# The last four chunks' expert lists: 24 list columns held stationary while the one-hot rows move

## The chip, the cores and the metric

The kernel runs on one core of a Trainium2 chip. The time is the device time of one execution in microseconds (us), the median of three runs. The core has a matrix engine (TensorE, PE in the profile; its weight loads are PEld), a vector engine (VectorE, DVE), a scalar engine (ScalarE, ACT), GpSimd (POOL) and SyncE (SP), which here only starts transfers. Each works through its own queue in order and waits on semaphores for the others.

## The reference

A gated linear attention makes one row of 384 numbers for each of 3072 tokens; a top-1 mixture of eight experts then works on these rows.

```python
for t in range(S):                      # attention; B, H, S, D = 4, 8, 768, 48
    S_re, S_im = (ar * S_re - ai * S_im) + kv, ar * S_im + ai * S_re
    y[:, :, t] = np.einsum('bhd,bhde->bhe', q[:, :, t], S_re)
x = y.transpose(0, 2, 1, 3).reshape(B * S, H * D)        # 3072 x 384

logits = x @ w_gate                                      # experts; E = 8, F = 1024
e_idx = np.argmax(logits, axis=1)
gate_w = softmax(logits)[np.arange(N), e_idx]
eom = 1.0 / (1.0 + np.exp(-(x @ w_output_gate)))
for e in range(E):
    mask = e_idx == e
    h = np.maximum(x[mask] @ w1[e], 0.0)
    out[mask] = gate_w[mask, None] * eom[mask, e, None] * (h @ w2[e])
```

## The kernel before, in words

Tokens are handled in 24 chunks of 128. The first half of the program is the attention; the second half computes the experts, in the order of how many tokens they hold, on fixed capacities of 464 rows for the first down to 384 for the last.

**Lists.** Each expert needs the list of its tokens: for each place (slot) in it the token's number and its gate. `choose` finds a token's expert and its rank in that expert's list, `weigh` its gate (two exponentials on ACT and six small operations on DVE). For the first 20 chunks the pair is scattered into a table in DRAM and read back into `slots` (four tiles of 116 slots for each expert) and `whole` (three tiles of 128 slots for the last expert). The last four chunks (`T0` onward) come too late for this way. Their part is added with matmuls, in `add`: `hot` is a one-hot matrix of 128 tokens by 464 slots for each chunk, `lhs` holds 24 columns for each token (for each expert the number, and the gate in a high and a low part), and their product, summed over the four chunks, is what `slots` and `whole` still lack. Then `slot_ids` makes the row numbers `sid`, and `gather` fetches the second expert's rows by them: four indirect transfers that POOL issues.

**Where it stands in the program.** All this happens while the first expert (expert 0) is being computed; its rows are put together by another way (`fill`) and need no list. An expert takes eight steps `ft`. A step has nine matmuls of 464 columns into `up` (L1235), from which ACT makes `hh` (L1239) and DVE makes `hl` (L1240), then nine into three accumulators `acc` (L1172): for each accumulator two that read `hh` and one that reads `hl`. The steps are shifted: the nine of `acc` for step n come behind the nine of `up` for step n+1. I call them up0, up1, acc0, up2, acc1 and so on. Meanwhile the next expert's weights arrive in pieces of 768 KB (`raw`, two buffers), and are split into a high part on ACT (L210) and a low part on DVE (L211). A `raw` buffer is free, and SP starts the next transfer, when DVE has made its third low part. The next expert's rows are transposed late in the expert (`xt`, L94).

The generator `lists` is advanced by one `yield` after each step of expert 0, so where it yields decides between which instructions of ACT and DVE its work is put: on these two engines the order is that of the program. On PE the order around expert 0 is chosen by the scheduler from the dependences.

```python
if loaded and e == 0:
    next(last, None)
    if ft == 3:
        over(lpool, lambda: ps.tile([P, 512], F32, name="yp", bufs=1))
```

Here `last` is `lists`, and `over` is a small test whether some expert holds more tokens than its capacity (one matmul L1390, one transpose). The list matmuls and `over` share one bank of PSUM, `yp`.

Of the kernel before, what the change touches and what calls it, by code (L numbers as in the profile page):

```python
# [10 lines left out]
F32 = mybir.dt.float32  # L11
F32R = mybir.dt.float32r
# [4 lines left out]
ALU = mybir.AluOpType  # L17
# [4 lines left out]
P = 128  # L22

CAPS = (464, 440, 424, 416, 408, 400, 392, 384)
CAP = max(CAPS)
# [9 lines left out]
def tile_gated_attention_moe(  # L35
# [216 lines left out]

    def choose(pool, bank, c0, n, tag=""):
        def small(name, shape, dt=F32):
            return pool.tile([P] + shape, dt, name=name + tag)
        gl = logits[:, c0:c0 + n, 0:E]
# [84 lines left out]
    def attention(wctx):  # L341
        with ExitStack() as actx:
# [404 lines left out]
            def place(c0, n):  # L747
                pool = ready["pool"]
                steps = choose(pool, bank, c0, n, tag=str(c0))
                next(steps)  # L750

                ohp = pool.tile([P, n, E], F32, name=f"ohp{c0}")
# [4 lines left out]
                dl, oh = at_once(steps)  # L757
                tail["choice", c0] = dl, oh, ohp
                for c in range(c0, c0 + n):
# [5 lines left out]

            def add(pool, bank):
                lp = bank()
                new = lp[:, :NS * 3 * E].rearrange("p (s x) -> p s x", x=3 * E)
                new_whole = lp[:, NS * 3 * E:(NS + KT) * 3 * E].rearrange("p (k x) -> p k x", x=3 * E)
                for i in range(NS):  # L770
                    for c in range(T0, NT):
                        nc.tensor.matmul(
                            new[:NP, i, :], tail["hot", c][:, i * NP:(i + 1) * NP], lhs[:, c - T0, :],
                            start=(c == T0), stop=(c == NT - 1))
                for c in range(T0, NT):
                    whole_hot = pool.tile([P, KT, NS, P // NS], F32R, name="whole", bufs=2)
                    nc.vector.tensor_scalar(
                        out=whole_hot,
                        in0=iota.rearrange("p (b n) -> p b n", b=NS)[:, :, :KT * P // NS].rearrange(
                            "p b (k a) -> p k b a", k=KT),  # L780
                        scalar1=rank[:, c:c + 1], scalar2=None, op0=ALU.is_equal)
                    for k in range(KT):
                        nc.tensor.matmul(
                            new_whole[:, k, :], whole_hot[:, k].rearrange("p b a -> p (b a)"),
                            lhs[:, c - T0, :], start=False, stop=(c == NT - 1), skip_group_check=True)
                for x in range(3):
                    at = slots[:NP, :, :, int(x > 0)]
                    nc.vector.tensor_tensor(
                        out=at, in0=at, in1=new[:NP, :, x * E:(x + 1) * E].rearrange("p s e -> p e s"), op=ALU.add)
                    at = whole[:, :, int(x > 0)]  # L790
                    nc.vector.tensor_tensor(out=at, in0=at, in1=new_whole[:, :, x * E + E - 1], op=ALU.add)

            def gates_of(pool, c0, n):
                dl, oh, ohp = tail["choice", c0]
                for _ in weigh(pool, c0, n, dl, oh, tag=str(c0)):
                    pass
                one = pool.tile([P, n, E], F32, name=f"one{c0}")
                l = lhs[:, c0 - T0:c0 - T0 + n, :]
                nc.vector.tensor_tensor(
                    out=one, in0=ohp, in1=entry[:, c0:c0 + n, 1].unsqueeze(2).broadcast_to([P, n, E]), op=ALU.mult)  # L800
                nc.vector.tensor_copy(out=l[:, :, E:2 * E], in_=one)
                nc.vector.tensor_tensor(
                    out=l[:, :, 2 * E:3 * E], in0=one, in1=l[:, :, E:2 * E].bitcast(F32), op=ALU.subtract)

# [119 lines left out]
            T0 = TAIL[0][0]  # L924
            group_of = {c: c0 for c0, n in TAIL for c in range(c0, c0 + n)}

# [99 lines left out]
            def lists(pool, bank):  # L1026
                for c in range(T0, NT):
                    c0 = group_of[c]
                    hot = tail["hot", c] = pool.tile([P, CAP], F32R, name=f"hot{c}")
                    nc.vector.tensor_scalar(out=hot, in0=iota, scalar1=rank[:, c:c + 1], scalar2=None, op0=ALU.is_equal)  # L1030
                    nc.vector.tensor_scalar(
                        out=lhs[:, c - T0, 0:E], in0=tail["choice", c0][2][:, c - c0, :], scalar1=entry[:, c, 0:1],
                        scalar2=None, op0=ALU.mult)
# [89 lines left out]
    def experts(ready, loaded=False):  # L1123
# [4 lines left out]
        with ExitStack() as ectx:  # L1128
# [93 lines left out]
            for e in range(E):  # L1222
# [5 lines left out]
                for ft in range(FT):  # L1228
# [239 lines left out]
```

## Time and profile before

| | us |
|---|---|
| median of three runs (lowest, highest) | 534.71 (533.62, 534.95) |
| the profiled execution's own time | 535.06 |
| its span, first to last instruction | 533.3 |
| PE busy | 495.2 (93%) |
| DVE busy | 340.6 (64%) |
| ACT busy | 314.2 (59%) |
| POOL busy | 116.3 (22%) |

The span is that of one execution recorded by the hardware profiler. Times in the rows are microseconds from its start. "Idle before" is how long the engine stood still ahead of an instruction, and the name behind the arrow is what it waited for. A row of the timeline merges instructions that follow each other; the end of a matmul is modelled, so the distance between two starts tells more than a row's own length.

### The profile page before, as it was taken

To read this page: it belongs to the slowest core of one execution; us is meant where nothing else is said; L and a number is where in the kernel's file an instruction comes from. 1 tells how busy PE (TensorE), PEld (TensorE's weight loads), DVE (VectorE), ACT (ScalarE), POOL (GpSimd) and SP (SyncE) were. 2 spreads that over 40 slices of the span, in tenths; PEclk is the share of its full clock that TensorE was granted. 3 is DMA by queue.
4 is the path that set the end of the run, shared out by engine and by line. 5 is a ranking of instruction groups with operands and counts; after the bars stand their busy time and mean duration, and the time that the engine had idled before them with its cause. 6 is when DMAs were issued, how large, how long until landed. Compare 5 with 4: busy or idle time off the path is not lost.

```text
span 533.3 us, 10970 instructions
## 1 busy us (share of the span) xinstructions
PE 495.2 (93%) x4191; PEld 427.8 (80%) x4191; DVE 340.6 (64%) x801; ACT 314.2 (59%) x581; POOL 116.3 (22%) x134
## 2 busy tenths in 40 slices
PE   2899896999989999999989899999999999999992
PEld 0378574877877878778787789999999999999992
DVE  5579678998877988898857646444353636355220
ACT  7678677887858789657624236355452726354220
POOL 4002002030110203033310544412334232111112
PEclk9799989999989999999999799999999999999998
DMA  8664542526235321104424565537163544431001
GB/s 285 199 216 137 120 132 61 164 67 179 72 75 149 45 77 49 29 31 135 143 56 145 161 170 180 165 82 235 44 205 120 173 149 142 142 115 50 15 27 45
DMA packets 46898, 63.84 MB, mean 120 GB/s; under 512 B 11769, under 2 KB 38668, under 8 KB 46836
## 3 DMA queue, kind: packets, MB, share of 16 engines
q1 hardware_dynamic: 38708, 53.63, 33.6%
q0 software_dynamic: 8128, 9.42, 6.2%
q8 instruction: 35, 0.57, 0.5%
q14 instruction: 27, 0.22, 0.2%
HBM read 53.92 MB, written 9.88 MB: 120 GB/s over the span
## 4 chain that ended last, share of the span: by engine, by line
PE 59%; issue 16%; DVE 8%; DMA 7%; ACT 5%; POOL 3%; POOLq 0%; SPq 0%; DVEq 0%; ACTq 0%
PE acc L1172 12%; PE up L1235 11%; PE tr L94 6%; PE sc L664 5%; PE cs L574 4%; PE xo L678 4%; PE tr L245 4%; PE cs L521 3%; POOL out_dram L1185 3%; PE xo L684 2%; DMA carry<-ai 2%; PE st L649 2%; DMA xd<-xn 1%; DMA ar<-in_a_re_dram 1%; DMA raw<-in_moe_w_dram 1%
## 5 line engine op out<-in xcount | busy, mean ns | idle before, releaser
L1240 DVE SCALAR_TENSOR_TENSOR hl<-up,hh 128x464 fp32r<-128x464 f32 (+7 forms) x64 | 37.7, 589 | 69.8 <-ACT hh L1239 69.5
L1239 ACT ACTIVATE hh<-up 128x464 fp32r<-128x464 f32 (+7 forms) x64 | 33.0, 516 | 72.5 <-PE up L1235 72.5
L1235 PE MATMUL up<-xh,w1h 128*128 128x464 f32 (+7 forms) x192 | 69.1, 360 | 0.2 <-ACT xh L1022 0.2
L1235 PE MATMUL up<-xl,w1h 128*128 128x464 f32 (+7 forms) x192 | 68.1, 355 | 0.0
L1235 PE MATMUL up<-xh,w1l 128*128 128x464 f32 (+7 forms) x192 | 67.8, 353 | 0.0
L1172 PE MATMUL acc<-hh,w2h 128*128 128x464 f32 (+6 forms) x168 | 61.8, 368 | 0.0
L1172 PE MATMUL acc<-hl,w2h 128*128 128x464 f32 (+6 forms) x168 | 59.8, 359 | 1.5 <-DVE hl L1240 1.5
L1172 PE MATMUL acc<-hh,w2l 128*128 128x464 f32 (+6 forms) x168 | 59.8, 356 | 0.0
L1185 POOL DMA_INDIRECT out_dram<-y,sid x28 | 31.7, 1134 | 125.2 <-ACT y L1207 122.2
L664 PE MATMUL sc<-qt,kt 96*128 96x128 f32 x384 | 52.4, 279 | 0.0
L664 PEld LDWEIGHTS sc<-qt,kt 96*128 96x128 f32 x384 | 47.2, 191 | 3.3 <-issue 1.7
L1116 POOL DMA_INDIRECT rows<-xd,sid x28 | 35.5, 1267 | 57.7 <-DVE w1l L211 29.2
L211 DVE TENSOR_TENSOR w1l<-raw,w1h 128x512 fp32r<-128x512 f32 x48 | 30.7, 685 | 18.9 <-ACT w1h L210 18.8
L678 PE MATMUL xo<-scores,v 128*48 128x128 f32 x384 | 42.7, 279 | 0.0
L211 DVE TENSOR_TENSOR w2l<-raw,w2h 128x512 fp32r<-128x512 f32 x48 | 30.6, 688 | 14.6 <-ACT w2h L210 14.3
L1062 POOL DMA_INDIRECT table<-entry,addr x20 | 28.1, 1404 | 53.5 <-DVE addr L1058 49.3
L1235 PEld LDWEIGHTS up<-xl,w1h 128*128 128x128 f32 x192 | 36.3, 189 | 1.6 <-DVE xl L1023 0.4
L210 ACT CAST w1h<-raw 128x512 fp32r<-128x512 f32 x48 | 27.1, 619 | 17.9 <-DMA raw<-in_moe_w_dram 17.9
L1235 PEld LDWEIGHTS up<-xh,w1h 128*128 128x128 f32 x192 | 36.5, 190 | 1.3 <-ACT xh L1022 0.4
L544 POOL COPY rcs<-rcs 24x48 f32<-24x48 f32 (+2 forms) x10 | 5.4, 540 | 146.2 <-DMA rcs<-re 95.6
L1235 PEld LDWEIGHTS up<-xh,w1l 128*128 128x128 f32 x192 | 36.4, 190 | 1.0
L684 PE MATMUL xo<-qt,state 96*48 96x128 f32 x320 | 36.7, 276 | 0.0
(213 smaller groups left out, 1117.9 us busy)
## 6 DMA issues: line engine op xcount, KB each, us to landing
raw<-in_moe_w_dram SPq DMA_DIRECT2D x32, 768.0 KB
ar<-in_a_re_dram SPq DMA_DIRECT2D x24, 192.0 KB
ai<-in_a_im_dram SPq DMA_DIRECT2D x24, 192.0 KB
k<-in_k_dram SPq DMA_DIRECT2D x24, 192.0 KB
q<-in_q_dram SPq DMA_DIRECT2D x24, 192.0 KB
v<-in_v_dram SPq DMA_DIRECT2D x24, 192.0 KB
xd<-xn SPq DMA_DIRECT2D x24, 192.0 KB
rows<-xd,sid POOLq DMA_INDIRECT x28, 4.3
```

The lines of the kernel that those rows point to most:

```text
L94: return nc.tensor.transpose(out=out, in_=in_, identity=ident[p0:p0 + n, p0:p0 + n])
L211: nc.vector.tensor_tensor(out=lo[:, s], in0=raw[:, s], in1=hi[:, s].bitcast(F32), op=ALU.subtract)
L664: nc.tensor.matmul(sp[:, j * P:(j + 1) * P], r["kt"][:D2, h, :], r["qt"][:D2, h, :], start=True, stop=True)
L678: nc.tensor.matmul(op[u * DP:u * DP + D, j * P:(j + 1) * P], vt[c][:, h * D:(h + 1) * D], r["s"][:, h, :], start=True, stop=(cc == 0))
L684: nc.tensor.matmul(op[u * DP:u * DP + D, j * P:(j + 1) * P], xs[:D2, h * D:(h + 1) * D], r["qt"][:D2, h, :], start=False, stop=True)
L1062: ins = nc.gpsimd.indirect_dma_start(out=table, out_offset=bass.IndirectOffsetOnAxis(ap=addr[:, c:c + 1], axis=0), in_=entry[:, c, :], in_ ...
L1116: ins = nc.gpsimd.indirect_dma_start(out=rows[e % 2][:n, i, :], out_offset=None, in_=xd[:known], in_offset=bass.IndirectOffsetOnAxis(ap=id ...
L1172: nc.tensor.matmul(accs[kt][:, :cap], w[:, cs], a, start=(ft == 0 and s == 0), stop=(ft == FT - 1 and s == 2))
L1185: ins = nc.gpsimd.indirect_dma_start(out=out, out_offset=bass.IndirectOffsetOnAxis(ap=id_of(e, i, n, loaded), axis=0), in_=y[:n, :], in_of ...
L1235: nc.tensor.matmul(up[:, :cap], w[:, kt, :], x[:, kt, :], start=(m == 0), stop=(m == 3 * KT - 1))
L1239: nc.scalar.activation(out=hh, in_=up[:, :cap], func=AF.Relu)
L1240: nc.vector.scalar_tensor_tensor(out=hl, in0=up[:, :cap], scalar=0.0, in1=hh.bitcast(F32), op0=ALU.max, op1=ALU.subtract)
```

## The change

Three things are done. First, the product is taken the other way round: `lhs` is stationary (24 columns) and a chunk's whole one-hot matrix moves (464 columns), four matmuls in place of 28, which leaves the result as 24 rows of 464 slots; these are copied out of PSUM twice (`by_slot` on ACT, and `by_whole`, which puts the last expert's slots in another order, on DVE) and turned by seven small transposes. The one-hot matrices for `whole` (four operations of 128x384 on DVE) go away. Second, the gates of the four chunks, which were computed in groups of two, one and one, are computed together. Third, `lists` has two more places where it yields, and `over` comes one step later. A loop that had four small operations for the first eight columns of `lhs` becomes one operation.

```diff
             def place(c0, n):
                 pool = ready["pool"]
-                steps = choose(pool, bank, c0, n, tag=str(c0))
+                if c0 == T0:
+                    for name in ("dl", "oh", "ohp"):
+                        tail[name] = pool.tile([P, NT - T0, E], F32, name=name + "s")
+                at = {name: tail[name][:, c0 - T0:c0 - T0 + n] for name in ("dl", "oh", "ohp")}
+                steps = choose(pool, bank, c0, n, tag=str(c0), at=at)
...
             def add(pool, bank):
+
+                W3, Q = 3 * E, P // NS
+                sp = bank()
+                for c in range(T0, NT):
+                    nc.tensor.matmul(
+                        sp[:W3, :CAP], lhs[:, c - T0, :], tail["hot", c], start=(c == T0), stop=(c == NT - 1))
+                by_slot = pool.tile([W3, CAP], F32, name="by_slot")
+                by_whole = pool.tile([W3, KT, NS, Q], F32, name="by_whole")
+                nc.scalar.copy(out=by_slot, in_=sp[:W3, :CAP])
+                nc.vector.tensor_copy(
+                    out=by_whole,
+                    in_=sp[:W3, :CAP].rearrange("p (b n) -> p b n", b=NS)[:, :, :KT * Q].rearrange(
+                        "p b (k a) -> p k b a", k=KT))
+                yield
                 lp = bank()
...
                 for i in range(NS):
-                    for c in range(T0, NT):
-                        nc.tensor.matmul(
-                            new[:NP, i, :], tail["hot", c][:, i * NP:(i + 1) * NP], lhs[:, c - T0, :],
-                            start=(c == T0), stop=(c == NT - 1))
-                for c in range(T0, NT):
-                    whole_hot = pool.tile([P, KT, NS, P // NS], F32R, name="whole", bufs=2)
-                    nc.vector.tensor_scalar(
...
-                    for k in range(KT):
-                        nc.tensor.matmul(
-                            new_whole[:, k, :], whole_hot[:, k].rearrange("p b a -> p (b a)"),
-                            lhs[:, c - T0, :], start=False, stop=(c == NT - 1), skip_group_check=True)
+                    turned(out=new[:NP, i, :], in_=by_slot[:, i * NP:(i + 1) * NP])
+                for k in range(KT):
+                    turned(out=new_whole[:, k, :], in_=by_whole[:, k].rearrange("p b a -> p (b a)"))
...
-            def gates_of(pool, c0, n):
-                dl, oh, ohp = tail["choice", c0]
-                for _ in weigh(pool, c0, n, dl, oh, tag=str(c0)):
-                    pass
...
+            def gates(pool):
+                n = NT - T0
+                yield from weigh(pool, T0, n, tail["dl"], tail["oh"], tag="s")
...
             def lists(pool, bank):
...
                 yield
-                for c0, n in TAIL:
-                    gates_of(pool, c0, n)
-                add(pool, bank)
+                for _ in gates(pool):
+                    pass
+                yield
+                yield from add(pool, bank)
                 slot_ids()
...
                         next(last, None)
-                        if ft == 3:
+                        if ft == 4:
                             over(lpool, lambda: ps.tile([P, 512], F32, name="yp", bufs=1))
```

What the program issues moves in three places. The first is PE in the middle of acc1, where the list matmuls begin; `hot_...` is the one-hot matrix of a chunk, `w2h` and `w2l` the two parts of the second weights. Before:

```order
L1172 MATMUL acc<-hh,w2l_3307 128x464
L772 MATMUL yp<-lhs,hot_3836 116x24
L772 MATMUL yp<-lhs,hot_3839 116x24
L1172 MATMUL acc<-hl,w2h_3306 128x464
L1172 MATMUL acc<-hh,w2h_3306 128x464
```

In the changed kernel the four list matmuls stand behind the last matmul of acc1 and ahead of up3:

```order
L1174 MATMUL acc<-hl,w2h_3306 128x464
L774 MATMUL yp<-hot_3830,lhs 24x464
L774 MATMUL yp<-hot_3832,lhs 24x464
L774 MATMUL yp<-hot_3834,lhs 24x464
L774 MATMUL yp<-hot_3836,lhs 24x464
L1237 MATMUL up<-xh_3775,w1h_3302 128x464
```

The first two of 28 list matmuls stood ahead of five matmuls of acc1; now all four stand behind them.

The second is PE in acc2, where before the rest of the list matmuls ran; `whole` is a one-hot matrix for the last expert. Before:

```order
L783 MATMUL yp<-lhs,whole 128x24 x3
L1172 MATMUL acc<-hh,w2h_3306 128x464
L783 MATMUL yp<-lhs,whole 128x24 x3
L1172 MATMUL acc<-hh,w2l_3307 128x464
L1172 MATMUL acc<-hh,w2h_3306 128x464
L1172 MATMUL acc<-hh,w2l_3307 128x464
L1390 LDWEIGHTS ones_b
L1390 MATMUL yp<-run,ones_b 128x8
L1172 MATMUL acc<-hl,w2h_3306 128x464 x3
```

In the changed kernel acc2 is whole, and the transposes stand between it and up4:

```order
L1174 MATMUL acc<-hh,w2h_3306 128x464
L1174 MATMUL acc<-hh,w2l_3307 128x464
L1174 MATMUL acc<-hl,w2h_3306 128x464
L94 MATMUL yp<-ident,by_slot 116x24 x4
L94 MATMUL yp<-ident,by_whole 128x24 x3
L1237 MATMUL up<-xh_3775,w1h_3304 128x464
```

The three matmuls that read `hl` no longer stand at the end of acc2, and `over`'s matmul has moved from inside acc2 to behind acc3.

The third is DVE, between the gates and the making of `sid`. Before, `hl` of step 2 and the rest of the weight split stood behind all of the list work:

```order
L802 TENSOR_TENSOR lhs<-one_3930,lhs 128x8
L777 TENSOR_SCALAR whole<-iota,rank 128x384 x4
L788 TENSOR_TENSOR slots<-slots,yp 116x32
L791 TENSOR_TENSOR whole<-whole,yp 128x3
...
L1095 TENSOR_SCALAR sid<-slots 116x32
L1039 TENSOR_SCALAR whole_sid<-whole 128x3
L1099 COPY gate<-slots 116x32
L211 TENSOR_TENSOR w1l_3849<-raw,w1h_3848 128x512
L211 TENSOR_TENSOR w2l_3853<-raw,w2h_3852 128x512
L1240 SCALAR_TENSOR_TENSOR hl<-up,hh 128x464
```

In the changed kernel they stand right behind the gates:

```order
L805 TENSOR_TENSOR lhs<-ones,lhs 128x4x8
L211 TENSOR_TENSOR w1l_3840<-raw,w1h_3839 128x512
L211 TENSOR_TENSOR w2l_3844<-raw,w2h_3843 128x512
L1242 SCALAR_TENSOR_TENSOR hl<-up,hh 128x464
L779 COPY by_whole<-yp 24x384
L211 TENSOR_TENSOR w2l_3844<-raw,w2h_3843 128x512 x2
L1242 SCALAR_TENSOR_TENSOR hl<-up,hh 128x464
L793 TENSOR_TENSOR slots<-slots,yp 116x32
```

`hl` of steps 2 and 3, and the third low part of the first weight piece, come ahead of the additions to `slots`. On ACT the exponentials of the four chunks shrink from six to two, and `by_slot` stands between `hh` of step 2 and the next two parts of the weight split. On POOL and SP the order is the same.

## Rows read from the trace of the kernel before

**Rows 1.** PE by line, 303.5 to 533.3 us: busy, mean; idle before

```profile
L1235 PE MATMUL up<-xh,w1h 128*128 128x440 f32 (+7 forms) x177 | 62.8, 355 | 0.0
...
L94 PE MATMUL yp<-ident,deep 128*1 128x128 f32 x1 | 0.3, 272 | 0.0
```

**Rows 2.** Timeline of PE, expert 0: start, length, engine, instruction

```profile
279.82 0.48 PE L1235 MATMUL up<-xh,w1h 128*128 128x464 f32 x1 [0.20 <-ACT xh L1022]
...
283.96 0.37 PE L1172 MATMUL acc<-hh,w2h 128*128 128x464 f32 x1
...
288.59 0.37 PE L1172 MATMUL acc<-hh,w2l 128*128 128x464 f32 x1
289.52 0.34 PE L772 MATMUL yp<-lhs,hot 128*116 128x24 f32 x2 [0.56 <-issue]
...
292.86 1.49 PE L772 MATMUL yp<-lhs,hot 128*116 128x24 f32 x13
...
294.88 0.45 PE L1172 MATMUL acc<-hh,w2h 128*128 128x464 f32 x1
...
296.05 0.43 PE L783 MATMUL yp<-lhs,whole 128*128 128x24 f32 x3
...
297.63 0.23 PE L1390 MATMUL yp<-run,ones_b 128*128 128x8 bf16 x1
299.37 1.53 PE L1172 MATMUL acc<-hl,w2h 128*128 128x464 f32 x3 [1.51 <-DVE hl L1240]
...
303.72 0.45 PE L1172 MATMUL acc<-hh,w2h 128*128 128x464 f32 x1
...
305.70 0.37 PE L1235 MATMUL up<-xh,w1h 128*128 128x464 f32 x1
```

**Rows 3.** Windows: length, busy PE PEld DVE ACT POOL, granted clock, DMA, GB/s

```profile
296.00:297.00 1.00, 1.00 (x6) 0.94 (x6) 0.49 (x5) 0.00 (x0) 0.00 (x0) 0.64 0.00 0
...
303.00:304.00 1.00, 1.00 (x6) 0.80 (x5) 0.00 (x0) 1.00 (x2) 0.87 (x1) 0.95 1.05 312
...
317.00:318.50 1.50, 1.50 (x13) 1.38 (x13) 0.00 (x0) 0.48 (x2) 0.11 (x1) 1.00 0.48 149
```

**Rows 4.** Timeline of DVE, expert 0

```profile
287.02 0.64 DVE L1240 SCALAR_TENSOR_TENSOR hl<-up,hh 128x464 fp32r<-128x464 f32 x1 [0.30 <-DMA xd<-xn]
287.58 0.17 DVE L296 TENSOR_TENSOR lo<-oh,logits 128x16 f32<-128x16 f32 x1
...
289.24 0.18 DVE L802 TENSOR_TENSOR lhs<-one,lhs 128x16 fp32r<-128x16 f32 x1
...
297.23 0.18 DVE L1095 TENSOR_SCALAR sid<-slots 116x32 uint32<-116x32 f32 x1
...
297.48 0.68 DVE L211 TENSOR_TENSOR w1l<-raw,w1h 128x512 fp32r<-128x512 f32 x1
```

**Rows 5.** Timeline of PE, the transposes of the second expert's rows

```profile
313.27 0.54 PE L94 MATMUL xt<-ident,rows 110*128 110x110 f32 x4
...
317.45 0.92 PE L94 MATMUL xt<-ident,rows 110*128 110x110 f32 x8
...
318.42 0.36 PE L1235 MATMUL up<-xh,w1l 128*128 128x440 f32 x1
```

**Rows 6.** Timeline of POOL, the second expert's gather, first and fourth

```profile
298.28 1.44 POOL L1116 DMA_INDIRECT rows<-xd,sid  x1 [29.19 <-DVE w1l L211]
...
303.13 1.07 POOL L1116 DMA_INDIRECT rows<-xd,sid  x1 [0.30 <-issue]
```

**Rows 7.** Gathers, issue to landing: the fourth alone, then all 31

```profile
DMA to landing us min/median/max: 4.9/4.9/4.9
...
DMA to landing us min/median/max: 2.9/4.2/11.6
```

**Rows 8.** Timeline of SP: the weight transfers of this stretch

```profile
298.19 2.75 SPq L194 DMA_DIRECT2D raw<-in_moe_w_dram  x2
```

**Rows 9.** Timeline of ACT: the first split of that piece

```profile
303.00 1.14 ACT L210 CAST w1h<-raw 128x512 fp32r<-128x512 f32 x2 [8.42 <-DMA raw<-in_moe_w_dram]
```

More of the change, by code (lines that the diff above doesn't have):

```diff
@@ L251, in gate_logits, with choose @@
             out=logits[:, i, :], in_=part[:, :, D2:].rearrange("p j x -> p x j"), axis=AX.X, op=ALU.add)
-    def choose(pool, bank, c0, n, tag=""):
+    def choose(pool, bank, c0, n, tag="", at=None):
         def small(name, shape, dt=F32):
-            return pool.tile([P] + shape, dt, name=name + tag)
+            return at[name] if at and name in at else pool.tile([P] + shape, dt, name=name + tag)
         gl = logits[:, c0:c0 + n, 0:E]
@@ L748, in place @@
                 pool = ready["pool"]
-                steps = choose(pool, bank, c0, n, tag=str(c0))
+                if c0 == T0:
[3 more added lines that the diff above has]
+                steps = choose(pool, bank, c0, n, tag=str(c0), at=at)
                 next(steps)
-                ohp = pool.tile([P, n, E], F32, name=f"ohp{c0}")
+                ohp = at["ohp"]
                 nc.vector.tensor_tensor(
@@ L756, in place @@
                 yield
-                dl, oh = at_once(steps)
-                tail["choice", c0] = dl, oh, ohp
+                at_once(steps)
                 for c in range(c0, c0 + n):
@@ L767, in add @@
+                nc.vector.tensor_copy(
[3 more added lines that the diff above has]
+                yield
                 lp = bank()
-                new = lp[:, :NS * 3 * E].rearrange("p (s x) -> p s x", x=3 * E)
-                new_whole = lp[:, NS * 3 * E:(NS + KT) * 3 * E].rearrange("p (k x) -> p k x", x=3 * E)
+                new = lp[:, :NS * W3].rearrange("p (s x) -> p s x", x=W3)
@@ L770, in add @@
+                new_whole = lp[:, NS * W3:(NS + KT) * W3].rearrange("p (k x) -> p k x", x=W3)
                 for i in range(NS):
-                    for c in range(T0, NT):
-                        nc.tensor.matmul(
-                            new[:NP, i, :], tail["hot", c][:, i * NP:(i + 1) * NP], lhs[:, c - T0, :],
-                            start=(c == T0), stop=(c == NT - 1))
-                for c in range(T0, NT):
-                    whole_hot = pool.tile([P, KT, NS, P // NS], F32R, name="whole", bufs=2)
-                    nc.vector.tensor_scalar(
[L778 to L781, printed above, removed]
-                    for k in range(KT):
-                        nc.tensor.matmul(
-                            new_whole[:, k, :], whole_hot[:, k].rearrange("p b a -> p (b a)"),
-                            lhs[:, c - T0, :], start=False, stop=(c == NT - 1), skip_group_check=True)
+                    turned(out=new[:NP, i, :], in_=by_slot[:, i * NP:(i + 1) * NP])
@@ L791, in add @@
                     nc.vector.tensor_tensor(out=at, in0=at, in1=new_whole[:, :, x * E + E - 1], op=ALU.add)
-            def gates_of(pool, c0, n):
-                dl, oh, ohp = tail["choice", c0]
-                for _ in weigh(pool, c0, n, dl, oh, tag=str(c0)):
-                    pass
-                one = pool.tile([P, n, E], F32, name=f"one{c0}")
-                l = lhs[:, c0 - T0:c0 - T0 + n, :]
+            def gates(pool):
+                n = NT - T0
+                yield from weigh(pool, T0, n, tail["dl"], tail["oh"], tag="s")
+                one = pool.tile([P, n, E], F32, name="ones")
                 nc.vector.tensor_tensor(
-                    out=one, in0=ohp, in1=entry[:, c0:c0 + n, 1].unsqueeze(2).broadcast_to([P, n, E]), op=ALU.mult)
-                nc.vector.tensor_copy(out=l[:, :, E:2 * E], in_=one)
+                    out=one, in0=tail["ohp"], in1=entry[:, T0:, 1].unsqueeze(2).broadcast_to([P, n, E]), op=ALU.mult)
+                nc.vector.tensor_copy(out=lhs[:, :, E:2 * E], in_=one)
                 nc.vector.tensor_tensor(
-                    out=l[:, :, 2 * E:3 * E], in0=one, in1=l[:, :, E:2 * E].bitcast(F32), op=ALU.subtract)
+                    out=lhs[:, :, 2 * E:3 * E], in0=one, in1=lhs[:, :, E:2 * E].bitcast(F32), op=ALU.subtract)
             FIXED = NT + 9
@@ L924, in attention @@
             T0 = TAIL[0][0]
-            group_of = {c: c0 for c0, n in TAIL for c in range(c0, c0 + n)}
             def rest():
@@ L1027, in lists @@
                 for c in range(T0, NT):
-                    c0 = group_of[c]
                     hot = tail["hot", c] = pool.tile([P, CAP], F32R, name=f"hot{c}")
                     nc.vector.tensor_scalar(out=hot, in0=iota, scalar1=rank[:, c:c + 1], scalar2=None, op0=ALU.is_equal)
-                    nc.vector.tensor_scalar(
-                        out=lhs[:, c - T0, 0:E], in0=tail["choice", c0][2][:, c - c0, :], scalar1=entry[:, c, 0:1],
-                        scalar2=None, op0=ALU.mult)
+                nc.vector.tensor_tensor(
+                    out=lhs[:, :, 0:E], in0=tail["ohp"],
+                    in1=entry[:, T0:, 0].unsqueeze(2).broadcast_to([P, NT - T0, E]), op=ALU.mult)
                 yield
-                for c0, n in TAIL:
-                    gates_of(pool, c0, n)
-                add(pool, bank)
+                for _ in gates(pool):
+                    pass
+                yield
+                yield from add(pool, bank)
                 slot_ids()
```

## The prediction

> **What bounds the kernel now.** I first read PE by line over the second half of the program. From 303.5 us to the end PE never waits: its twelve groups all show 0.0 us of idle time, from the largest to the smallest [rows 1]. So whatever moves PE's position at 303.5 us moves the end of the program by as much, as long as PE's inputs keep up. The change lies just ahead of that point, so I read the timeline of PE from the first matmul of expert 0 on, to see how much of that stretch is not expert work [rows 2].
>
> The unit is a matmul of 464 columns. From 283.96 to 288.59 us there are 22 in an undisturbed row (acc0, up2 and four of acc1): 4.63 / 22 = 0.2105 us each. From 279.82 (up0) to 305.70 us (the first of up5) there are 81 of them (up0 to up4 and acc0 to acc3). They should take 17.05 us and take 25.88, so 8.83 us are something else [rows 2]. By stretches, each less 0.2105 us for every 464-column matmul in it:
> - 279.82 to 283.96, 18 matmuls: 0.35, the start behind `xh`.
> - 288.59 to 292.86, 14 matmuls: 1.32, the wait for the first `lhs` (0.56 as idle), three list matmuls and the restarts behind them.
> - 292.86 to 294.88: 2.02, nineteen list matmuls.
> - 294.88 to 297.63, six matmuls: 1.49, the last six list matmuls, and a lower clock at the end.
> - 297.63 to 299.37: 1.74, the wait for `hl` of step 2, with `over`'s small matmul in it.
> - 299.37 to 303.72, twelve matmuls: 1.82, the lower clock.
> - 303.72 to 305.70, nine matmuls: 0.09, a restart.
>
> The windows confirm the clock: 0.64 on average from 296 to 297 us and 0.95 from 303 to 304 [rows 3]. [...] Ahead of the fall PE did a long run of 24-column matmuls (292.86 to 294.88 and in between until 296.3).
>
> **The change, step by step.** *List matmuls.* Gone are 28, with their restarts. In their place are four that move 464 columns. The trace has none with 24 stationary columns; I take the price of the 464-column matmul, 4 x 0.2105 = 0.84, and 0.09 for the restart: 0.93 us. It can't be much less while the columns stream, and at most it is the 0.11 us of weight load more for each (19 in 2.02 us [rows 2] is 0.106), so 0.9 to 1.4.
>
> *Transposes.* Seven, of 24 columns. The nearest row is eight transposes of 110 columns: from 317.45 to 318.42 they and one 440-column matmul (0.20) take 0.97 us, so 0.096 each, restart included [rows 5]. Seven take 0.67; the bounds are 0.3 (less to move) and 0.74 (the 0.106 us of the old list matmuls).
>
> *`over`* keeps its matmul and its transpose, one step later, between matmuls that need nothing of it: 0.1 each, 0.2.
>
> *The wait for `lhs`.* PE reaches the list matmuls at 283.96 + 27 x 0.2105 = 289.64. On DVE the gates begin behind `hl` of step 1, which ends a wait for an old transfer at 287.02 and is not touched; the first group's chain ran from 287.58 to 289.42 [rows 4]. Now the same ten steps carry 32 columns in place of 16; I allow 0.1 more, 289.5. Hidden by 0.1 us; were each step 0.05 longer, PE would wait 0.4.
>
> *The wait for `hl` of step 2.* Behind the gates DVE now has two splits and `hl`: 0.68 + 0.68 + 0.64 [rows 4], done at 291.5. PE asks for it at the third matmul of acc2: 289.64 + 0.93 + 11 x 0.2105 = 292.9. The 1.74 us go, with 1.4 to spare. The gates' second and third group, the four `whole` operations and three small ones only leave DVE sooner; I count nothing for them.
>
> *The copies.* No row shows a 24-row copy; `hl` reads 464 columns of PSUM in 0.64 [rows 4], so I take 0.64 each, from 0.3 to 1.3. `by_slot` starts at about 290.8, `by_whole` behind it, done at 292.1 (293.4 at worst); PE wants them at 289.64 + 0.93 + 18 x 0.2105 = 294.36. Hidden. Behind `by_whole` on DVE stand two splits and `hl` of step 3, done by 294.2 (295.5); acc3 reads it at 297.3. Behind `by_slot` on ACT stand two splits and `hh` of step 3, with as much room.
>
> *The weight piece.* The third low part of the first piece moves from 297.48 to 289.5 on DVE, so SP can start the third transfer at 290.2 in place of 298.19 [rows 4, 8]. It took 4.8 us to its first use at 303.00, for which ACT had stood idle 8.42 us [rows 8, 9]; that now comes at 295.0, and two splits (1.14) clear ACT before up4 ends at 296.9.
>
> *The clock.* What went ahead of the fall, 28 matmuls of 24 columns and two waits, shrinks to 0.67 us of transposes with no wait beside it. Elsewhere eight transposes in a row left the clock at 1.00 [rows 3, 5]. I take no fall.
>
> The new extras are 0.35 + 0.93 + 0.67 + 0.2 = 2.15 us against 8.83: a gain of 6.68. Against the profiled execution's own 535.06 us this gives 528.4; that execution lies 0.35 above the median of 534.71, so the median becomes 528.0. I add 0.1 for `lhs`: **528.1 us**.
>
> *The gather, which decides whether PE keeps the gain.* PE comes to the transposes `xt` at 313.27 - 6.68 = 306.6 and to the fourth tile's 0.3 later, 306.9 [rows 5]. But `sid` doesn't move as far: it came 0.75 us behind the end of the last list matmul (296.05 + 0.43) [rows 2, 4]; the last transpose will end at about 295.2, so it comes 1.25 earlier. The fourth gather is issued at 301.9 and lands, with 4.9 us as before, at 306.8; with the median of all gathers, 4.2, at 306.1 [rows 6, 7]. So the slack, more than 5 us before, is almost used up. Before, the gather shared full queues with two weight pieces (DMA share 1.05 [rows 3]); now these two are done by then. I count no wait.
>
> **The rivals.** *The clock falls again.* A spell as long as before, 6.8 us at half speed with PE busy throughout, costs 3.4 us: 531.4. For it speaks that the fall came in this very place behind small matmuls, against it what is said above. [...]
>
> *The gather lands late.* Each microsecond beyond 5.0 from issue to landing is one that PE waits. At 6 to 8 us it costs 1 to 3: 529 to 531. At the slowest of all, 11.6 [rows 7], it costs 6.6 and the kernel is where it was, 534.6.
>
> *Slower.* The third weight piece comes very late. ACT works in order, and `hh` of step 4 stands behind two splits of that piece; PE needs that `hh` for acc4 at 300.9. If the piece lands at X, PE waits X + 1.7 - 300.9. Up to 299.2 nothing is seen; at 305.9 the gain is gone, and the kernel is slower by 0.3% (536.3) at 307.5, 17 us behind its issue against 4.8 now. The early start is new, but the queues were empty just ahead of the old one (share 0.00 from 296 to 297 us [rows 3]).
>
> **How the numbers follow.** About 0.3%, 1.6 us, can be told from no change. Chances: 75% for the forecast, by itself 527.3 to 528.9 (list matmuls and transposes at their bounds, runs spread by 0.7); 11% for a gather that costs 0.3 to 4 us; 8% for the clock; 4% for a gather that eats the gain; 2% for the slower one. So faster 0.94, same 0.04, slower 0.02. The range goes from 527.1 to 531.0: it takes in most of the mild gather cases and leaves out about 17%.
>
> **What would show it.** In the changed profile: four matmuls L774 0.21 apart starting at about 289.65 us; no idle time of PE behind `hl` between 289 and 300; the granted clock 1.00 from 292 to 304; seven transposes in 0.7 us; acc3 starting at 297.0 in place of 303.72; the third `raw` transfer starting at about 290; `xt` at 306.6 with no idle time ahead of it. Wrong would be the forecast if PE stood ahead of `xt`, if the clock fell behind the transposes, or if PE had idle time behind 303 us that was 0.0 before.

## The result and the profile after

The changed kernel takes 527.47 us, the median of four runs (526.95 to 535.07), against 534.48 us for the kernel before on the same chip (four runs, 533.62 to 534.95). The ratio is 0.9867, with a 95% interval from 0.9848 to 0.9887: faster by 1.3%. One of the four runs (535.07) was a disturbed one and is left out of the ratio; the median of the other three is 527.10. The profiled execution took 527.84 us, its span is 526.1 us.

The timeline of PE, from the first matmul of expert 0 to the second expert's rows (start, length, instruction, idle before):

```profile
277.12 0.48 PE L1237 MATMUL up<-xh,w1h 128*128 128x464 f32 x1 [0.19 <-ACT xh L1024]
...
286.97 1.01 PE L774 MATMUL yp<-hot,lhs 128*24 128x464 f32 x4
287.81 0.38 PE L1237 MATMUL up<-xh,w1h 128*128 128x464 f32 x1
...
290.12 0.37 PE L1174 MATMUL acc<-hl,w2h 128*128 128x464 f32 x1
...
291.38 0.37 PE L1174 MATMUL acc<-hl,w2h 128*128 128x464 f32 x1
291.68 0.40 PE L94 MATMUL yp<-ident,by_slot 24*116 24x24 f32 x4
291.93 0.34 PE L94 MATMUL yp<-ident,by_whole 24*128 24x24 f32 x3
292.52 0.37 PE L1237 MATMUL up<-xh,w1l 128*128 128x464 f32 x1
...
294.21 0.37 PE L1174 MATMUL acc<-hh,w2h 128*128 128x464 f32 x1
...
303.94 0.45 PE L94 MATMUL xt<-ident,rows 110*128 110x110 f32 x3
305.83 0.31 PE L94 MATMUL xt<-ident,rows 110*128 110x110 f32 x1 [1.44 <-DMA rows<-xd,sid]
```

From `up0` to the first `xt` the time was 313.27 - 279.82 = 33.45 us [rows 2, 5]; now it is 303.94 - 277.12 = 26.82 us, so 6.63 us less. The four list matmuls take 0.84 us in all. Between the start of the last matmul of acc2 (291.38) and the second matmul of up4 (292.52) lie 1.14 us, of which two matmuls are 0.42: the seven transposes with their restart cost 0.72. No wait for `lhs` or `hl` is left, and acc3 starts at 294.21, 17.09 us behind `up0` (forecast 297.0 - 279.82 = 17.18). But at 305.83 there is a new one: PE stands 1.44 us for the last tile of the gather.

The windows (length, busy PE, granted clock, DMA share, GB/s) answer to [rows 3]:

```profile
292.00:293.00 1.00, 1.00 (x9) 1.00 0.60 192
...
296.00:297.00 1.00, 1.00 (x7) 1.00 0.50 129
...
288.00:320.00 32.00, 30.57 (x159) 1.00 0.58 162
```

The clock is 1.00 through the whole stretch. On DVE the gates, `hl` of step 2, the copy and `sid` (before: [rows 4]):

```profile
284.05 0.64 DVE L1242 SCALAR_TENSOR_TENSOR hl<-up,hh 128x464 fp32r<-128x464 f32 x1 [0.46 <-DMA xd<-xn]
284.61 0.18 DVE L296 TENSOR_TENSOR los<-ohs,logits 128x32 f32<-128x32 f32 x1
...
286.34 0.19 DVE L805 TENSOR_TENSOR lhs<-ones,lhs 128x32 fp32r<-128x32 f32 x1
...
287.66 0.63 DVE L1242 SCALAR_TENSOR_TENSOR hl<-up,hh 128x464 fp32r<-128x464 f32 x1
288.58 0.55 DVE L779 COPY by_whole<-yp 24x384 f32<-24x384 f32 x1 [0.29 <-ACT by_slot L778]
...
293.03 0.18 DVE L1097 TENSOR_SCALAR sid<-slots 116x32 uint32<-116x32 f32 x1
```

The gather on POOL (before: [rows 6, 7]), with the time from issue to landing of the transfer at 298.55:

```profile
294.07 1.44 POOL L1118 DMA_INDIRECT rows<-xd,sid  x1 [27.69 <-DVE w1l L211]
...
298.55 1.23 POOL L1118 DMA_INDIRECT rows<-xd,sid  x1 [0.30 <-issue]
...
DMA to landing us min/median/max: 7.2/7.2/7.2
```

And the weight transfers that SP starts (before: [rows 8]):

```profile
287.16 0.40 SPq L194 DMA_DIRECT2D raw<-in_moe_w_dram  x1
290.42 0.40 SPq L194 DMA_DIRECT2D raw<-in_moe_w_dram  x1
298.73 0.38 SPq L194 DMA_DIRECT2D raw<-in_moe_w_dram  x1
300.95 0.37 SPq L194 DMA_DIRECT2D raw<-in_moe_w_dram  x1
```

The pieces of 287.16 and 290.42 are the two that started at 298.19 and 300.54 before. Those of 298.73 and 300.95 are the third expert's first two: they start right behind the issue of the gather's last tile. In the kernel before the first of them came 3.5 us behind that issue (at 303.13):

```profile
306.66 0.38 SPq L194 DMA_DIRECT2D raw<-in_moe_w_dram  x1
```

The span is 7.2 us shorter, and these parts make it up. `up0` starts 279.82 - 277.12 = 2.70 us earlier, and that isn't the change's doing: in the profiles below the kernel before starts it at 276.83 and the changed kernel at 278.25 and 280.39. The stretch to `xt` gives 6.63. The wait at the gather takes 1.66 of that (from the first `xt` to the next set 5.84 us, against 4.18 before). Behind the next set 0.47 more is lost.

### The profile page after: what moved, and what is told of

It is laid out like the page before. It is cut to its first block, busy times and chain, and to the rows that moved or that the text cites. A ratio compares the mean times of both kernels' runs of the same rounds, so it can differ in the third digit from the quotient of the medians.

```text
span 526.1 us, 10906 instructions
## 1 busy us (share of the span) xinstructions
PE 489.5 (93%) x4174; PEld 422.7 (80%) x4174; DVE 336.2 (64%) x777; ACT 314.6 (60%) x578; POOL 115.9 (22%) x134
## 4 chain that ended last, share of the span: by engine, by line
PE 56%; issue 16%; DVE 10%; DMA 7%; ACT 5%; POOL 4%; POOLq 0%; SPq 0%; DVEq 0%; ACTq 0%
PE up L1237 12%; PE acc L1174 11%; PE tr L94 6%; PE sc L664 4%; PE cs L574 4%; PE tr L245 3%; PE xo L678 3%; POOL out_dram L1187 3%; PE cs L521 3%; DMA carry<-ai 3%; PE xo L684 2%; PE st L649 2%; DMA rows<-xd,sid 1%; DMA raw<-in_moe_w_dram 1%; DMA ar<-in_a_re_dram 1%
## 5 line engine op out<-in xcount | busy, mean ns | idle before, releaser
L665 DVE TENSOR_TENSOR scores<-sc,mask 128x512 f32<-128x512 f32 x48 | 32.6, 682 | 5.1 <-PE sc L664 4.6
```

Of the source, the lines that this page charges most:

```text
L665: nc.vector.tensor_tensor(out=r["s"][:, 4 * hh:4 * hh + 4, :], in0=sp.rearrange("p (h t) -> p h t", t=P), in1=mask.unsqueeze(1).broadcast_ ...
```

## The experiments

My theory: the gain has three sources that depend on each other. PE no longer waits, the list takes fewer instructions, and because of both the clock doesn't fall. A part of the gain is given back, since the gather's last tile now meets the third expert's weights in the transfer queues. Rivals: one of the two edits (gates together, product turned) brings nearly all, or each brings its own share whatever the other does; the clock's fall is chance; the wait at the gather is chance. For the clock there were two theories: that a fall needs PE to stand still, or that narrow matmuls alone bring it about.

The experiments were timed in five rounds, f_long in three; times are compared between kernels of one chip only (e_gates, e_swap and c1_after on one, e_oneadd, e_hold and e_small on another, f_after, f_oneadd, f_both and f_burst on a third, f_long on a fourth). In the table "to `xt`" is from the start of `up0` to the first `xt`, "wait" is PE's idle time before the fourth `xt`, "rest" is from `up0` to the end of the span, all in us of the profiled execution. A star marks a spell at half clock that began 0.8 to 1.1 us behind `up0`, long before the list work, and lasted 3.4 us: some 1.6 us of that row's "to `xt`" are from it (28.38 - 26.81 in f_both).

| kernel | ratio to before (95%) | up0 | to xt | wait | rest |
|---|---|---|---|---|---|
| before, first profile | | 279.82 | 33.45 | 0 | 253.48 |
| c0_before | 1.0012 (0.9978 to 1.0047) | 276.83 | 34.89 | 0 | 255.27 |
| changed, first profile | 0.9867 (0.9848 to 0.9887) | 277.12 | 26.82 | 1.44 | 248.98 |
| c1_after | 0.9889 (0.9838 to 0.9941) | 278.25 | 26.80 | 1.15 | 248.65 |
| f_after | 0.9880 (0.9824 to 0.9937) | 280.39 | 26.81 | 1.01 | 249.01 |
| e_gates | 0.9933 (0.9898 to 0.9968) | 276.72 | 32.12 | 0 | 252.78 |
| e_swap | 0.9956 (0.9920 to 0.9993) | 276.79 | 32.89 | 0 | 253.11 |
| e_oneadd | 0.9906 (0.9870 to 0.9942) | 279.07 | 26.88 | 0 | 247.33 |
| f_oneadd | 0.9859 (0.9797 to 0.9921) | 279.94 | 26.81 | 0 | 247.06 |
| e_hold | 0.9862 (0.9808 to 0.9915) | 281.20 | 26.82 | 0 | 247.30 |
| f_both | 0.9899 (0.9853 to 0.9945) | 282.22 | 28.38* | 0 | 248.58 |
| e_small | 0.9905 (0.9868 to 0.9942) | 279.26 | 29.54* | 1.46 | 251.24 |
| f_burst | 0.9945 (0.9910 to 0.9981) | 281.75 | 30.43* | 0 | 250.65 |
| f_long | 1.0027 (0.9976 to 1.0079) | 277.63 | 34.74* | 0 | 254.77 |

**The two kernels again** (c0_before, c1_after; f_after on a third chip).

> The kernel before, unchanged, profiled and timed again, because its one profiled execution lost 2.9 us in the attention part (150 to 161 us, a late carry transfer and a spell of half clock) that the profile of the changed kernel did not lose. If that loss is chance of one execution, up0 of expert 0 starts anywhere from 277 to 280 us here. If it belongs to the kernel (its memory layout, which the change alters), up0 starts at 279.8 again. Both expect ratio 1.000, and the stretch from up0 to acc3 within 0.2 us of its 23.9.

> The changed kernel, unchanged, profiled and timed again. Chance theory: up0 starts at 277 to 280 us as in the kernel before; the layout theory: at 277.1 again. The stretch from up0 to acc3 should be 17.1 us again under both. The wait of 1.44 us of PE for the fourth gather ahead of the transposes xt belongs to the change (list numbers come only 1.3 us sooner while PE comes 6.7 sooner): 0.5 to 3 us again; the rival, that it was a disturbance of one execution, expects none.

> The changed kernel again, for the comparison on this chip. From the first matmul of expert 0 to the first transpose of the second expert's rows 26.8 us, PE's idle time there 1.0 to 1.5 us, the rest of the span after the first matmul of expert 0 248.6 to 249.0 us, ratio to before 0.987 to 0.989.

The stretch to `xt` repeats within 0.02 us in the changed kernel, and the wait at the gather is there each time, so in this kernel it isn't chance. In the kernel before the stretch is 1.4 us longer on repeating. That missed the expectation (within 0.2 us up to acc3), while the start of `up0` at 276.83 spoke for the chance theory. The clock is why: PE's waits there are no longer than before (0.43 us for `lhs` and 1.50 for `hl`, against 0.56 and 1.51), but it is low from 292.4 to 302.6 us (0.69 in the first of these windows: 0.62 us of it at 0.5), ten us:

```profile
292.00:293.00 1.00, 1.00 (x6) 0.69 0.00 0
302.00:303.00 1.00, 1.00 (x5) 0.69 1.11 332
```

The first profile showed 6.8: 0.72 us of the first window of [rows 3], the six windows that follow it, and 0.10 us of the second. The first and the last of the six:

```profile
297.00:298.00 1.00, 0.86 (x4) 0.50 0.00 0
...
302.00:303.00 1.00, 1.00 (x4) 0.50 1.00 304
```

**One edit at a time.** In e_gates the gates of the four chunks are together, with the new `yield` and `over` one step later, but `add` is the 28 matmuls of before (the cut shows the call; against the changed kernel):

```diff
...
-                yield from add(pool, bank)
+                add(pool, bank)
```

> Gates together, the new yields and over one step later, but the old 28 list matmuls and the whole one-hots. My theory (the hl wait and its half clock came from the order on DVE): the wait of 1.5 us for hl is gone, list work costs 28 x 0.106 + 0.4 = 3.4 us in place of 1.6; without a fall of the clock 4.9 us faster than before, 529.6 or ratio 0.991. The rival, that the run of 24-column matmuls is what makes the clock fall: a spell of half clock behind the list matmuls as before, and up to 3.4 us less gain, 531 to 533.

In e_swap only the product is turned; the gates stay in their three groups, `add` runs in one go, and `over` stays at step 3 (the cut shows the call; against the kernel before):

```diff
...
-                add(pool, bank)
+                for _ in add(pool, bank):
+                    pass
```

> The new list matmuls, copies and transposes alone; gates in three groups, everything of the list in one go on DVE and ACT as before, over at its old place. My theory: PE still waits for the third lhs, for the copies and for hl of step 2, about 1 us each; gain 3 to 4 us without a fall of the clock, 0.5 to 2 with one, so ratio 0.993 to 0.999. The rival, that the operand swap is what the gain comes from: ratio 0.987 as in the changed kernel.

Against the first profile of before, whose spell at half clock was as long as in these two (6.8 us), they shorten the stretch to `xt` by 1.3 and 0.6 us alone, and the changed kernel shortens it by 6.6; against c0_before, with its longer spell, it is 2.8 and 2.0 alone and 8.1 in c1_after. In both the clock falls. In e_swap PE still stands (0.80 us for `lhs`, 0.79 for `by_whole`, 0.32 for `hh`, 0.57 for `hl`). In e_gates the wait for `hl` is gone and PE stands 0.25 us in all between 286 and 290 us, and the fall comes all the same. Timeline and windows of e_gates:

```profile
286.81 1.76 PE L775 MATMUL yp<-lhs,hot 128*116 128x24 f32 x16
288.43 0.46 PE L1235 MATMUL up<-xh,w1h 128*128 128x464 f32 x1
289.03 0.50 PE L786 MATMUL yp<-lhs,whole 128*128 128x24 f32 x3
```

```profile
288.00:289.00 1.00, 0.88 (x7) 1.00 0.75 57
289.00:290.00 1.00, 0.97 (x7) 0.88 0.72 276
290.00:291.00 1.00, 1.00 (x6) 0.50 1.05 408
...
296.00:297.00 1.00, 1.00 (x4) 0.70 0.63 149
```

In e_swap it falls at 293.4 us and rises at 300.3:

```profile
293.00:294.00 1.00, 1.00 (x6) 0.71 0.00 0
...
300.00:301.00 1.00, 1.00 (x6) 0.87 1.15 348
```

In these profiles neither edit brings the whole gain alone. The timed runs too show less for each edit alone, but not that the two depend on each other: on this chip e_gates is 0.7% faster than the kernel before, e_swap 0.4%, and c1_after, with both, 1.1%, so there the two shares add up. The intervals in the table are too wide to decide it; that the whole is worth more than its parts rests on one profile of each edit. e_gates holds the new `yield` behind the gates and the later `over` too; which of them removes the wait for `hl` was not tried by itself.

**What makes the clock fall.** Each of these is the changed kernel with more narrow work just ahead of the seven transposes, written to a part of the bank that nothing reads. e_small has 21 more transposes:

```diff
+                for i in range(21):
+                    spare = lp[:, (NS + KT + i % 7) * W3:(NS + KT + i % 7 + 1) * W3]
+                    turned(out=spare[:NP], in_=by_slot[:, i % NS * NP:(i % NS + 1) * NP])
```

> The changed kernel with 21 more transposes of 24 columns into spare columns of the bank (28 in place of 7; the extra ones are read by nothing). They take 21 x 0.074 = 1.6 us of PE, and the wait ahead of xt (1.3 us) should shrink by as much, so by work alone the time is that of the changed kernel within 0.5 us. If a run of small matmuls is what makes the clock fall, with no wait beside it, the granted clock shows 0.50 for 6 us or more behind them, and up0 to xt grows from 26.8 us to 31 or more, 3 us slower in all. If the fall needed the old waits, the clock stays at 1.00.

f_burst has 21 matmuls of the old form in their place, and f_long 49 (`range(49)`):

```diff
+                for i in range(21):
+                    spare = lp[:, (NS + KT + i % 7) * W3:(NS + KT + i % 7 + 1) * W3]
+                    nc.tensor.matmul(
+                        spare[:NP], tail["hot", T0][:, i % NS * NP:(i % NS + 1) * NP], lhs[:, 0, :], start=True, stop=True)
```

> The changed kernel with 21 more matmuls of 24 columns just ahead of the seven transposes, each with 128 rows and 116 columns of a one-hot matrix stationary, into a part of the bank that nothing reads. They take the place where 21 more transposes left the clock at 1.00. Theory A (it is the kind of work: matmuls whose weight load sets the pace, 0.106 us each): 2.2 us for the 21, and the granted clock falls behind them for 6 to 10 us, which costs 3 to 5 us more, so 5 to 7 us above the changed kernel in all. Theory B (it was the short stops around them in the kernel before, or chance): only the 2.2 us, clock 1.00.

> The changed kernel with 49 more matmuls of 24 columns in place of the 21 that left the clock at 1.00: the same work in the same place, about 5.2 us of it and then the seven transposes, about as long as the stretch of list matmuls with their stops in the kernel that kept the old product (5.6 us, where the clock fell after 3.4 us). Theory A (the length of a stretch with hardly any wide matmuls decides): the granted clock falls within the block or behind it, the last of the narrow matmuls come more slowly, and some 10 us above the changed kernel in all. Theory B (the stops between the narrow matmuls decide): the clock stays at 1.00, 5.2 us more for the block, less what the gather's wait gives back (1.0 to 1.4 us), so 4 to 5 us above the changed kernel.

The narrow work of e_small, and the window around it:

```profile
295.38 1.58 PE L94 MATMUL yp<-ident,by_slot 24*116 24x24 f32 x25
296.81 0.34 PE L94 MATMUL yp<-ident,by_whole 24*128 24x24 f32 x3
```

```profile
288.00:320.00 32.00, 30.54 (x172) 1.00 0.51 147
```

The clock stays at 1.00 behind 28 transposes in a row (1.7 us). The wait ahead of `xt` didn't shrink as expected: it is 1.46 us, since `sid`, and with it the gather, comes behind the transposes and moves with them. The clock stays at 1.00 too behind f_burst's 21 matmuls and seven transposes, 2.7 us in all:

```profile
297.79 2.21 PE L789 MATMUL yp<-lhs,hot 128*116 128x24 f32 x21
```

```profile
288.00:320.00 32.00, 32.00 (x176) 1.00 0.47 141
```

In f_long it falls. Its timeline and windows:

```profile
293.64 5.05 PE L789 MATMUL yp<-lhs,hot 128*116 128x24 f32 x49
298.63 0.41 PE L94 MATMUL yp<-ident,by_slot 24*116 24x24 f32 x4
298.88 0.49 PE L94 MATMUL yp<-ident,by_whole 24*128 24x24 f32 x3
299.30 0.76 PE L1241 MATMUL up<-xh,w1h 128*128 128x464 f32 x1
```

```profile
298.00:299.00 1.00, 1.00 (x13) 0.94 0.00 0
299.00:300.00 1.00, 1.00 (x6) 0.50 0.00 0
...
302.00:303.00 1.00, 1.00 (x5) 0.85 0.00 0
```

PE hasn't stood for a moment there (1.00 busy in each window from 293 us on), and the clock goes to 0.50 from about 298.9 to 302.3 us. So in f_long the fall came behind narrow matmuls alone, without a stop of PE. In e_swap, with no narrow list matmul but seven transposes and several waits, it falls too (0.50 from 294 to 300 us), so there it came without them. The changed kernel has neither, and in all seven profiles with its list work (three of the kernel itself, e_oneadd, f_oneadd, e_hold and f_both) the clock stays at 1.00 behind it. The theory that only the stops matter falls. In size f_long was nearer to theory B: to `xt` it takes 34.74 - 26.81 = 7.9 us more, of which the star is 1.6, the block 5.0 and the fall 1.3, since the spell was only 3.4 us long; and PE doesn't wait for the gather.

What isn't shown is how much narrow work is safe. f_burst and f_long were profiled once each. In c0_before and e_gates the clock fell 2.65 and 2.95 us behind the start of the long run of list matmuls, about as long as f_burst's 2.7 us that left it alone. And the same work, just ahead of `up0`, was followed by a fall in the four profiles with a star and by none in the other ten.

**The gather.** e_oneadd and f_oneadd (the same kernel) take away the `yield` inside the list's addition, so that the transposes come 2.4 us behind the list matmuls in place of 4.7:

```diff
-                yield from add(pool, bank)
+                for _ in add(pool, bank):
+                    pass
```

> The changed kernel with one yield fewer: the copies, the transposes and the additions to slots come in one go on DVE, and PE gets the seven transposes inside up3. My theory: sid comes 2 us sooner, the fourth gather lands ahead of the transposes xt, the wait of PE there (1.44 and 1.15 us in two executions) is gone and the kernel is 1 to 1.4 us faster than the changed one: 526 to 527 where that has 527.5 to 528.5. The rival, that the gather's landing is set by the weight transfers beside it and not by its start: a wait of 1 us or more stays.

> The changed kernel without the yield inside the list's addition. Theory (the fourth gather lands late because it is issued late behind a busy queue): PE waits nothing at the row transposes, span after the first matmul of expert 0 247.3 us, so 1.3 to 1.6 us (0.25 to 0.3%) less than the changed kernel on the same chip. Rival (the idle time is chance from one execution to the next): both the same within 0.1%.

e_hold leaves the list as it is and holds the third expert's weight transfers back until the gather's last tile has landed:

```diff
-                gather(1, CAPS[1])
+                ready["gathered"] = gather(1, CAPS[1])
...
-        pieces_of = lambda e: load_pieces(stage, who[e] if loaded else e)
+        pieces_of = lambda e: load_pieces(
+            stage, who[e] if loaded else e, ready.get("gathered") if loaded and e == 2 else None)
```

> The changed kernel, with the four weight pieces of the third expert held back until the second expert's gather has landed. If the fourth gather lands late (7.2 us) because it shares the queues with these pieces, it now lands after 3.4 to 4.5 us and PE doesn't wait ahead of xt: 1.2 us faster than the changed kernel, unless the held pieces are late themselves. If the gather is slow by itself, the wait stays at 1.1 to 1.5 us.

f_both has both edits.

> Both remedies for the gather at once: no yield inside the addition, and the third expert's weight transfers held back behind the gather. If the gather's wait is all that either takes away, it is no better than either alone: span after the first matmul of expert 0 247.3 us. If holding back the weights makes them late for ACT, PE shows idle time behind hh of a later step and the span grows by what it shows.

Either edit takes the wait away. e_hold issues the last tile as late as the changed kernel does (21.45 us behind `up0`, against 298.55 - 277.12 = 21.43), only the weights come later. They start at 306.24, 3.6 us behind the issue, so the tile had landed by then; in the changed kernel that took 7.2. The rows of e_hold, SP's next weight transfers, POOL's last tile and PE's `xt`, without idle time:

```profile
306.24 1.02 SPq L194 DMA_DIRECT2D raw<-in_moe_w_dram  x2
...
302.65 1.22 POOL L1118 DMA_INDIRECT rows<-xd,sid  x1 [0.30 <-issue]
...
308.02 0.54 PE L94 MATMUL xt<-ident,rows 110*128 110x110 f32 x4
```

So in this pair the late landing comes of the weight transfers beside it: in the five us behind the issue the DMA share is 0.61 to 1.08 in the changed kernel, and 0.16 to 0.53 here. POOL's tile lands 7.2 us behind its issue with SP's weights beside it (the changed kernel), and within 3.6 us without (e_hold).

The meeting doesn't cost PE a wait every time. In f_burst the last tile and the two weight transfers behind it stand to each other and to the fourth `xt` as in the changed kernel (weights 0.2 and 2.4 us behind the issue, the fourth `xt` due 5.6 us behind it), the DMA share is 0.51 to 1.15, and PE waits for nothing, so that tile landed within 5.6 us:

```profile
306.81 1.22 POOL L1122 DMA_INDIRECT rows<-xd,sid  x1 [0.30 <-issue]
...
306.98 2.58 SPq L194 DMA_DIRECT2D raw<-in_moe_w_dram  x2
...
312.18 0.54 PE L94 MATMUL xt<-ident,rows 110*128 110x110 f32 x4
```

The changed kernel's three profiles and e_small show the wait. What made the difference in f_burst is open. In f_oneadd the tile is issued 19.5 us behind `up0`, ahead of the weights (299.44 against 301.55):

```profile
299.44 1.06 POOL L1119 DMA_INDIRECT rows<-xd,sid  x1 [0.30 <-issue]
...
301.55 0.38 SPq L194 DMA_DIRECT2D raw<-in_moe_w_dram  x1
...
306.75 0.54 PE L94 MATMUL xt<-ident,rows 110*128 110x110 f32 x4
```

The stretch from `up0` to the end is 247.06 to 247.33 us in e_oneadd, f_oneadd and e_hold, 248.65 to 249.01 in three profiles of the changed kernel: 1.3 to 1.9 us are to be had. Of this the gather's wait, with what follows it, is 1.2 to 1.7 us (from the first `xt` to the next set 5.41 to 5.84 us, in place of 4.18); what lies behind that set took 215.8 to 216.8 us over all fourteen profiles, whatever the kernel. The times don't settle it: on one chip f_oneadd has 528.00 us (median) and the changed kernel 530.14, but f_both, whose wait is gone as well, has 531.37, and the intervals of the ratios overlap. The 526 to 527 us expected of e_oneadd were missed (532.62, on a chip where the kernel before takes 536.59). So that f_oneadd is faster than the changed kernel is shown by the stretch and not by the times. f_both is no better than either alone: 248.58, less the 1.6 of its star, is 247.0.

## Why the prediction was right

The forecast was 528.1 us, the time is 527.47. Its steps against the profile:

- *What bounds the kernel.* Right: what PE gains in expert 0 the end gains, except for what the gather takes and the spread of the part behind it (0.47 us here).
- *The extras.* Forecast 2.15 us between `up0` and `xt`; measured 0.36 (start, 4.15 us for 18 matmuls), 0.84 (list), 0.72 (transposes with restart) and 0.24 (`over`), 2.16 in all. The gain to `xt` was to be 6.68 and is 6.63. Single terms were off by 0.09 at most: the list matmuls, which move as many columns as their neighbours, show no restart.
- *The wait for `lhs`.* Right, with more to spare: the gates end at 286.53, PE asks at 286.97. The chain on 32 columns took 1.92 us against 1.84 on 16. The spare is 0.44 in place of 0.1 because `hl` of step 1 came 6.93 us behind `up0` and not 7.20. The 0.1 that I added was not needed.
- *The wait for `hl` of step 2.* Right: done at 288.29, asked for at 290.12.
- *The copies.* Hidden, as said; 0.54 and 0.55 us against 0.64.
- *The third weight piece.* It starts at 287.16, 10.04 us behind `up0` (forecast 10.38). ACT stands 1.07 us for it, PE doesn't.
- *The clock.* Right in the forecast that it stays up, in seven profiles of seven. The reason given, less narrow work and no wait beside it, is borne out in direction by f_long, f_burst and e_small (5.2 us of narrow work and a fall, 2.7 and 1.7 us and none), with one profile of each. The rival, a spell as long as the 6.8 us of the first profile before, now behind the seven transposes, did not come. That transposes bring a fall gets no support from e_small, where 28 in a row left the clock at 1.00. It isn't refuted: the row was 1.7 us long, 2.7 us that were mostly list matmuls (f_burst) left it at 1.00 too, and in e_swap the seven transposes stand between two waits just ahead of the fall.
- *The gather.* **This step failed:** "I count no wait". PE waits 1.0 to 1.4 us in three profiles of three, so the rival "the gather lands late" (11%) happened beside the forecast. The issue was even a little earlier than forecast (21.43 us behind `up0`, forecast 22.08), but the tile took 7.2 us to land in place of 4.9. By the rival's own price (each microsecond beyond 5.0) that is 2.2 us, less 0.65 for the earlier issue, 1.55, and PE stood 1.44. The sentence behind the mistake is that the two weight pieces "are done by then". They are, but the same rule (a buffer is free when DVE has made its third low part) moves the *next* two pieces forward as well, and they meet the gather's last tile. The first of them starts 21.61 us behind `up0`, where it was 26.84, and 0.18 us behind the issue of the last tile, where it was 3.5. I followed the earlier start through one transfer and not through the next.
- *The total.* That it came out so close is partly luck: with the 1.66 us of the gather put in, the forecast's own sum gives 529.8, 2.3 us more than was measured. By the mechanisms alone the first profile gives 6.63 - 1.66 = 5.0 us. The other 2.2 of the span are the earlier start of `up0` (2.70, less 0.47 lost at the end). The start of `up0` lies between 276.7 and 282.2 us over all profiles, in kernels that do the same work in the attention part. Against c0_before, with its longer spell at half clock, the mechanisms give 34.89 - 26.80, less 1.4 at c1_after's gather (5.54 us between the two sets of `xt` in place of 4.18), 6.7. So the median's gain, 7.0 us in the first comparison and 6.0 and 4.7 in two later ones, is of the size that the mechanisms give. That it varies with the spell is likely but not shown, since the spell is known only of the profiled executions.

## What to carry to other kernels

The product with few output columns was cheap in the trace's single rows (0.106 us a matmul) and dear in what stood around it (in before, waits of 0.56 and 1.51 us and 6.8 us at half clock): turned so that the wide side moves, 28 matmuls became four of 0.21 us and, with the waits gone too, the clock stayed at 1.00 in seven profiles of seven. Two edits that each seem to bring little in a profile may be worth more together, if a wait and the clock both have to go before either shows; test them together before one is dropped, and compare the timed runs too, which here showed two shares that add up (0.7%, 0.4%, both 1.1%). When a change frees a buffer earlier, follow *all* transfers that wait on that chain of buffers, and ask what each of them meets in the queues; here the same gather issued 1.9 us earlier left PE no wait.

## What the runs showed of the hardware

- In f_long the clock fell while PE was busy throughout: 1.00 busy in each window from 293 to 300 us, and the granted clock at 0.50 from 298.9. PE had done 5.2 us of 24-column work. Behind 2.7 us of the same (f_burst) it stayed at 1.00. Each is one profile.
- The spells at half clock were not of one length: 3.4 us in f_long, 6.8 in before, e_gates and e_swap, 10.2 in c0_before. The stretch to `xt` of the kernel before was 33.45 us in one execution (before) and 34.89 in another (c0_before).
- In four of fourteen profiles (the stars) there was a spell right behind `up0` as well. PE had stood 0.96 us for a one-hot row and 0.19 for `xh` just ahead of it, and it stood as long in the ten profiles that show no such spell. What decides it is open.
- 24 stationary columns didn't slow a matmul of 464 moving columns: 0.21 us (four in 0.84, in the changed kernel), as with 128 (nine in 1.89, from 287.81 to 289.70 us there). A transpose of 24 columns with 24 rows stationary took 0.06 us in a row (25 in 1.43, from start to start, in e_small), a list matmul of 24 columns with 128 rows stationary 0.10 (49 in 4.99, in f_long).
